# Attention and MLP block: lone score batches laid out one slot to a bank, the last v tile's products moved past the other projections, and the orders around them rewritten

## Chip, core and metric

The kernel runs on one core of one Trainium2 chip. The metric is the device time of one execution in microseconds (us). Three runs of the kernel before are given. The profile is of one further execution.

## What is computed

A block over S = 2048 tokens of width D = 640, all in float32, with adaptive LayerNorm (six vectors from `silu(c) @ w_mod`), sliding-window attention (32 heads of 20, window 256) and an MLP of width 1536. Cut to what matters:

```python
sa, ca, ga, sb, cb, gb = split(silu(c) @ w_mod)          # six vectors of 640
h = layernorm(x) * (1 + ca) + sa
q, k, v = heads(h @ wqkv)                                 # 32 heads of 20
p = softmax(where(0 <= i - j < 256, q @ k.T * 20**-0.5, -1e9))
x = x + ga * ((p @ v) @ wo)
h = layernorm(x) * (1 + cb) + sb
x = x + gb * (gelu(layernorm(h) @ w1 + b1) @ w2 + b2)
```

## The kernel before

**Numbers.** Each large product runs as three passes, high part times high part, low times high and high times low, so a float32 operand stands as two tiles, such as `hhi` and `hlo`. Making such a pair takes a copy on ScalarE (ACT) and a subtraction on GpSimd (POOL) or VectorE (DVE).

**Head.** The first two 512-token chunks are normalised, turned on TensorE (PE, tiles `psx`), scaled by `sa` and `ca1`, and the first q and k tiles are made from them (`pp`). `modulate(j)` makes `sa` and `ca1` for one fifth of the features. The string `ORDER` is the order, written out by hand, in which the head's pieces are issued: T turn, L the low part, P products, M `modulate`, S and N statistics and normalising. `run(RUN0)` is a row of dummy products (`warm`).

**The loop.** Its step t issues for one group of four heads (a quad) and one 128-query block the scores with the keys along the free axis (`s`, whose maximum gives the softmax's shift, `nm`). `LAG` = 11 steps behind it come the scores again with the queries along the free axis (`e`), a mask on DVE, the exponential on ACT (`pt`), and two zeroing selects on POOL. Two steps later follows `pt` times v (`o`, copied to `oT`). So steps 0 to 10 have an `s` batch alone, steps 11 to 127 have both, and steps 128 to 138 have an `e` batch alone. A batch is four heads of 384 columns. Two heads work on rows 0 to 63 of the PE array and two on rows 64 to 127. `score_banks` gives a batch 4 x 384 columns in three 512-column PSUM banks. So `cuts` splits the two middle heads at a bank's edge, and `score_batch` lets the second half of the array wait (a no-op with a dependence) before it writes a bank that the other half has written. Eight banks are there: three for `s`, three for `e`, one for `o`, one for `p`. Small results go "aside" into one of them.

**What fills the steps.** Between the batches stand the products of the remaining q, k and v tiles for the four chunks, 15 of 512 columns to a unit. `UNITS` is their sequence. `lay_units` spreads them so that they end by step `LAST` = 112, with a number per step that `EXTRA` shifts. Other tables place the weights' splits (`EARLY`), the asides (`AFTER`), the order of the `oT` copy against the exponential (`SUMS_LAST`) and the engine of a subtraction (`LOV`, `MV`). At step `TOMID` = 113 the projections' memory is given to the next part (`open_mid`). The output projection (`wo`) of the first four 128-row blocks stands in steps 116 to 138, placed by `TAIL_AT`. `MODS` places the sums that make the vectors ga, cb, sb and gb, on DVE, in the loop.

**Rows.** q and k go to DRAM and come back as rows of `qbuf` and `kbuf`, of which there are `NSLOT` = 4. The first rows of a quad that is due at step d are issued at step d - 7 (q) and d - 6 (k), or once they are written and their slot is free.

**MLP.** Four chunks, each 12 tiles of 128, every tile with 15 products `h`, a gelu on ACT, and 15 products `out`. The remaining 12 blocks of the output projection are placed between them.

**Issue.** All engines run their instructions in the order of the program. SyncE (SP) issues nearly all DMAs, also in program order.

## Time and profile before

| | |
|---|---|
| runs | 1003.28, 1004.44, 1005.43 us, median 1004.44 |
| the profiled execution | 1003.39 us, its span 1001.7 us |
| mean granted TensorE clock | 0.985 |
| PE busy | 952.5 us (95%) |
| DVE, POOL, ACT busy | 585.6, 495.4, 445.5 us |
| moved by DMA | 152.89 MB, mean 153 GB/s |

A row of the timeline gives start, duration, engine, operation, tiles, shape and count. In brackets is the idle time of that engine just before, and what ended it. A PE row with several instructions runs from the first start to the last end. Ends of products are modelled and overlap the next start, so what an instruction takes of PE's time is the distance from start to start. Float32 products that are not split count as two instructions. "PEclk" or "clock" is the granted share of the TensorE clock.

### The profile page before, as it was taken

Reading aid. Unit: us, or ns where it says so; the run is one execution under the profiler, and the core shown is the slowest. Engines: PE = TensorE matmul, PEld = TensorE weight load, DVE = VectorE, ACT = ScalarE, POOL = GpSimd, SP = SyncE. Lnnn points to the kernel's source line nnn. Section 1 sums busy time; section 2 is a strip of 40 time slices with the busy share of each in tenths; the row PEclk is TensorE's granted clock in tenths of the full one; section 3 lists DMA queues with packets and bytes.
Section 4 is the critical chain, followed back from the end, with each engine's and each line's share of the span. In section 5 each row is a group of like instructions: output and inputs, shape, how many; then the busy total and the mean of one; then the engine's idle time right before and its main releaser. Section 6 shows DMA issues by size and latency. Waiting matters only on the chain.

```text
span 1001.7 us, 19961 instructions
## 1 busy us (share of the span) xinstructions
PE 952.5 (95%) x7712; PEld 754.9 (75%) x7712; DVE 585.6 (58%) x929; ACT 445.5 (44%) x784; POOL 495.4 (49%) x695
## 2 busy tenths in 40 slices
PE   7899999999999999999988879999999999999997
PEld 7677677776777777777666658888888888888886
DVE  6753867768766788777778654655434343433112
ACT  3733545565654445554545554343433343333122
POOL 4323656577764355544536744454554546442221
PEclk8999999999999999999979999999999999999999
DMA  8375777655687477844582133544422334124113
GB/s 301 106 238 142 250 217 259 193 151 189 200 252 221 128 247 234 253 127 166 144 224 69 50 90 114 149 142 133 133 86 84 97 121 133 40 63 148 53 45 114
DMA packets 99429, 152.89 MB, mean 153 GB/s; under 512 B 8904, under 2 KB 42312, under 8 KB 99336
## 3 DMA queue, kind: packets, MB, share of 16 engines
q1 hardware_dynamic: 90120, 143.24, 47.0%
q10 hardware_dynamic: 9216, 8.39, 2.6%
q8 instruction: 61, 1.00, 0.4%
q14 instruction: 32, 0.26, 0.1%
HBM read 99.17 MB, written 51.58 MB: 150 GB/s over the span
## 4 chain that ended last, share of the span: by engine, by line
PE 80%; DVE 9%; ACT 5%; issue 2%; DMA 2%; POOL 1%; SPq 0%; ACTq 0%; DVEq 0%; POOLq 0%
PE h L119 16%; PE out L119 16%; PE pp L119 16%; PE o L119 7%; PE e L119 7%; PE wo L119 7%; PE s L119 6%; DVE e L119 4%; ACT pt L119 3%; DVE nm L119 2%; PE ppo L119 1%; DVE s L119 1%; PE yt L119 1%; PE xt L119 1%; DMA wc<-in_wcol 1%
## 5 line engine op out<-in xcount | busy, mean ns | idle before, releaser
L119 POOL TENSOR_SCALAR_AFFINE_SELECT pt<-pt 128x512 f32<-128x512 f32 x192 | 130.2, 678 | 148.2 <-ACT pt L119 141.6
L119 ACT ACTIVATE pt<-e 128x1024 f32<-128x1024 f32 (+1 forms) x120 | 133.8, 1115 | 54.0 <-DVE e L119 47.7
L119 DVE TENSOR_REDUCE nm<-s 128x4 f32<-128x1024 f32 (+1 forms) x128 | 152.6, 1192 | 4.4
L119 POOL TENSOR_TENSOR w2lo<-w2r,w2hi 128x640 fp32r<-128x640 f32 x48 | 75.8, 1578 | 158.2 <-ACT w2hi L119 158.0
L119 PEld LDWEIGHTS e<-qbuf,kbuf 62*128 62x128 f32 x792 | 84.9, 189 | 61.3 <-ACT pt L119 33.9
L119 PE MATMUL e<-qbuf,kbuf 62*128 62x128 f32 (+2 forms) x792 | 110.9, 319 | 19.9 <-ACT pt L119 17.2
L119 PE MATMUL pp<-hhi,whi 128*128 128x512 f32 x275 | 120.6, 439 | 2.3 <-ACT hhi L119 1.5
L119 PE MATMUL s<-kbuf,qbuf 60*128 60x256 f32 (+2 forms) x744 | 111.0, 311 | 7.5 <-DVE nm L119 5.8
L119 DVE CAST ghi<-g 128x512 fp32r<-128x512 f32 x48 | 25.8, 538 | 156.3 <-ACT g L119 156.2
L119 PE MATMUL pp<-hlo,whi 128*128 128x512 f32 x275 | 113.6, 413 | 2.4 <-POOL hlo L119 2.4
L119 DVE COPY_PREDICATED e<-mask_t,e 128x512 f32<-128x512 uint32 x96 | 66.6, 693 | 77.9 <-PE e L119 69.3
L119 PE MATMUL pp<-hhi,wlo 128*128 128x512 f32 x275 | 111.8, 407 | 0.0
L119 PE MATMUL o<-pt,vbuf 128*32 128x128 f32 x2688 | 101.7, 281 | 1.6 <-ACT xT L119 0.8
L119 POOL TENSOR_TENSOR wlo<-wraw,whi 128x128 fp32r<-128x128 f32 x185 | 81.6, 472 | 43.2 <-ACT whi L119 43.2
L119 PEld LDWEIGHTS s<-kbuf,qbuf 60*128 60x128 f32 x744 | 85.4, 188 | 19.8 <-PE pp L119 4.5
L119 ACT COPY oT<-o 128x128 f32<-128x128 f32 x128 | 33.9, 265 | 145.4 <-PE o L119 142.4
L119 PE MATMUL out<-ghi,w2hi 128*128 128x512 f32 x240 | 96.1, 400 | 0.0
L119 PE MATMUL h<-yhi,w1hi 128*128 128x512 f32 x240 | 95.6, 399 | 0.0
L119 PE MATMUL out<-ghi,w2lo 128*128 128x512 f32 x240 | 93.9, 391 | 0.0
L119 PE MATMUL out<-glo,w2hi 128*128 128x512 f32 x240 | 93.9, 391 | 0.0
L119 PE MATMUL h<-ylo,w1hi 128*128 128x512 f32 x240 | 93.8, 391 | 0.0
L119 PE MATMUL h<-yhi,w1lo 128*128 128x512 f32 x240 | 93.8, 391 | 0.0
(158 smaller groups left out, 1818.0 us busy)
## 6 DMA issues: line engine op xcount, KB each, us to landing
w2r<-in_w SPq DMA_DIRECT2D x48, 320.0 KB
qbuf<-q_scr SPq DMA_DIRECT2D x60, 240.0 KB
wraw<-in_wqkv SPq DMA_DIRECT2D x38, 320.0 KB
kbuf<-k_scr SPq DMA_DIRECT2D x44, 240.0 KB
q_scr<-stage SPq DMA_DIRECT2D x20, 512.0 KB
k_scr<-stage SPq DMA_DIRECT2D x20, 512.0 KB
o_scr<-oT ACTq DMA_DIRECT2D x64, 128.0 KB
wm<-in_wmod SPq DMA_DIRECT2D x20, 320.0 KB
```

The costliest lines, as they stand in the source:

```text
L119: return self.tc.keep_in_program_order(op(*args, **kw))
```

## The change

- **Lone batches.** Before step 11 the `s` tile, and from step 128 on the `e` tile, has four whole banks, one for each head, and no head is cut. The pools are closed and opened anew at steps 11 and 128 (`turn_scores`). Steps 11 to 127 keep three banks each.
- **The last v tile.** Its two units (30 products) leave the sequence. They run in steps 111 to 116 from the next part's memory (`late_units`). `LAST` goes from 112 to 108, `TOMID` from 113 to 110.
- **Gate.** The sums for gb leave the loop (steps 76 to 88). They stand in the first MLP chunk, with their five loads at the MLP's start (`gate`).
- **Memory.** `NSLOT` goes from 4 to 3, so the first rows of a quad are issued at step d - 5 (q) and d - 4 (k). The weights of the output projection get a pool of their own, and `yT` takes the place of `hT`.
- **Head.** `ORDER` is rewritten with further dummy products (R) in it, and `warm` goes from 31 to 61 in all, two of them in step 130 (`WARM`).
- **Tables.** `EXTRA`, `EARLY`, `AFTER`, `SUMS_LAST`, `LOV`, `HIA`, `MV`, `TAIL_AT` and others have other numbers. Four subtractions of the projections and four pairs of the modulation after the output projection go from POOL to DVE.

```diff
-NSLOT = 4
+NSLOT = 3
-RUN0 = 31
+RUN0 = 33
-    "T00 M1 S0 L00 S1 P00 S2 T01 S3 N L01 M2 T02 M3 P01 T10 T03 T11 L10 L02 M4 P02 C T04 L03 L11 P10 L04 T12 P03 T13 P11 "
+ORDER = ('T00 M1 L00 S0 S1 R12 S2 R3 S3 T01 M2 L01 P00 N T02 P01 M3 R3 T03 T10 L03 L02 M4 R1 T11 R1 R6 L10 C P02 T04 P10 ...
-LAST = 112
+LAST = 108
-EXTRA = {10: -2, 11: 2, 12: -1, 13: 1, 14: 1, 16: -3, ...
+EXTRA = {9: -2, 10: -2, 11: 6, 12: 1, 13: -1, 14: -2, ...
-MODS = [[9.25, 16.5], [18.0, 26.25], [68.5, 79.5], [76.75, 87.75]]
+MODS = [[9.5, 17.0], [16.75, 27.5], [70.5, 79.0]]
-TOMID = 113
+TOMID = 110
+WARM = {(130, 1): 2}
+LATE_AT = [110.25, 110.5, 110.5, 111.5, 113.25, 114.25, 116.5]
...
+    def turn_scores(t, n):
+        if t in (LAG, n):
+            sco_ctx.close()
+            for name in ("e", "s") if t == LAG else ("e",):
+                open_banks(name, sco_ctx)
...
-        t = pools[kind].tile([P, 4 * 384], F32, tag=kind, name=name)
-        return t, t.rearrange("p (h n) -> p h n", n=384)
+        n = width()
+        t = pools[kind].tile([P, 4 * n], F32, tag=kind, name=name)
+        return t, t.rearrange("p (h n) -> p h n", n=n)[:, :, 0:384]
+    def width():
+        return 384 if LAG <= now[0] < 2 * NQB * QUADS else 512
...
+    def late_units(key):
+        units = [unit(*key, c2, gp, acc, True) for c2 in range(2)]
+        def load():
+            w.append(box2["mid"].tile([P, KT, P], F32, tag="raw1", bufs=2, name="wraw_late"))
+            nc.sync.dma_start(w[0].rearrange("p k m -> p (k m)"), wqkv[key[1] * KT + key[2]])
+        def high():
+            nc.scalar.copy(w[1], w[0])
+        def low():
+            gp.tensor_tensor(w[2], w[0], f32(w[1]), ALU.subtract)
...
+    wm5 = [mp.tile([P, D], F32, name=f"wm5_{kt}") for kt in range(KT)]
+    for kt in range(KT):
+        nc.sync.dma_start(wm5[kt], wmod[5, kt])
+    def gate(i):
+        if i < KT:
+            mod_sum(wm5[0], wm5[i], i)
...
+            if ch == 0 and f > 1:
+                gate(f - 2)
```

Three places show what the new order does. First PE at step 2, where the `s` batch of the third query block (`s0_0_2`) stands alone between two projection units (`ppo1`, `pp0_1_1`). Before:

```order
L119 MATMUL ppo1_579<-hhi1_344,wlo001_519 128x512
L119 MATMUL s0_0_2_613<-kbuf0_97,qbuf0_93 128x256
L119 MATMUL s0_0_2_613<-kbuf0_97,qbuf0_93 128x384
L119 MATMUL s0_0_2_613<-kbuf0_97,qbuf0_93 128x128 x2
L119 MATMUL s0_0_2_613<-kbuf0_97,qbuf0_93 128x384
L119 MATMUL s0_0_2_613<-kbuf0_97,qbuf0_93 128x256
L119 MATMUL pp0_1_1_625<-hhi0_245,whi011_602 128x512
```

Now, at the same place:

```order
L119 MATMUL ppo1_602<-hhi1_371,wlo001_546 128x512
L119 MATMUL s0_0_2_636<-kbuf0_99,qbuf0_96 128x384 x4
L119 MATMUL pp0_1_1_645<-hhi0_246,whi011_625 128x512
L119 MATMUL pp0_1_1_645<-hlo0_247,whi011_625 128x512
L119 MATMUL pp0_1_1_645<-hhi0_246,wlo011_626 128x512
```

Six products became four, and the one wait inside the batch is gone. The lone `e` batches of steps 128 to 138 change in the same way. Second, PE in step 112, between the `o` products and the next `e` batch (`e1_4_6`). Before, only the turned maxima (`pm`) stand there:

```order
L119 MATMUL o1_4_2_6518<-pt1_4_1_6312,vbuf2_103 32x128 x4
L119 MATMUL o1_4_2_6518<-pt1_4_2_6362,vbuf2_103 32x128 x4
L119 MATMUL o1_4_2_6518<-pt1_4_3_6408,vbuf2_103 32x128 x4
L119 MATMUL pm1_5_6540<-idn_61,nm1_5_6054 32x128
L119 MATMUL e1_4_6_6550<-qbuf0_93,kbuf0_97 128x256
```

Now eight products of the last v tile (`pp_late`) do:

```order
L119 MATMUL o1_4_2_6467<-pt1_4_3_6358,vbuf2_104 32x128 x4
L119 MATMUL pp_late_6440<-hhi2_2369,wlo_late_6387 128x512
L119 MATMUL pp_late_6440<-hhi2_2369,whi_late_6386 128x512
L119 MATMUL pm1_5_6490<-idn_61,nm1_5_6034 32x128
L119 MATMUL pp_late_6440<-hlo2_2370,whi_late_6386 128x512
L119 MATMUL pp_late_6440<-hhi2_2369,wlo_late_6387 128x512
L119 MATMUL pp_late_6440<-hhi2_2369,whi_late_6386 128x512
L119 MATMUL pp_late_6440<-hlo2_2370,whi_late_6386 128x512
L119 MATMUL pp_late_6440<-hhi2_2369,wlo_late_6387 128x512
L119 MATMUL pp_late_6440<-hhi2_2369,whi_late_6386 128x512
L119 MATMUL e1_4_6_6506<-qbuf0_96,kbuf0_99 128x256
```

Counted over the steps in this order, the projections' products per step were 10, 5, 5, 10, 0, 0, 0, 0, 0 in steps 108 to 116. Now they are 0, 0, 0, 5, 8, 2, 5, 7, 3. Steps 11 to 107 hold 655 of them before and after. Third, SP's queue at the MLP's start, where `w1r2` and `w1r3` are raw tiles of the MLP's first weight and `w2r1` one of its second. Before:

```order
L119 DMA xb4_7757<-in_x 128x640
L119 DMA w1r2_7977<-in_w1 128x640
L119 DMA x1_scr<-xT3_7828 128x5x128
L119 DMA w1r3_7981<-in_w1 128x640
L119 DMA w2r1_7985<-in_w2 128x640
```

Now the gate's five loads, into memory that the attention's v tiles held, stand ahead of them:

```order
L119 DMA x1_scr<-xT3_7778 128x5x128
L119 DMA wm5_0_7932<-in_wmod 128x640
L119 DMA wm5_1_7933<-in_wmod 128x640
L119 DMA wm5_2_7934<-in_wmod 128x640
L119 DMA wm5_3_7935<-in_wmod 128x640
L119 DMA wm5_4_7936<-in_wmod 128x640
L119 DMA w1r2_7942<-in_w1 128x640
L119 DMA w1r3_7946<-in_w1 128x640
L119 DMA w2r1_7950<-in_w2 128x640
```

`w1r2` moved behind five loads and behind the store of `xT3`.

## The prediction

> **What bounds the kernel now.** I read the page first, for the span and TensorE's share.

> ```profile
> span 1001.7 us, 19961 instructions
> PE 952.5 (95%) x7712; PEld 754.9 (75%) x7712; DVE 585.6 (58%) x929; ACT 445.5 (44%) x784; POOL 495.4 (49%) x695
> ```

> PE is busy for 95% of the span, so time can go where PE's work shrinks, or where PE idles or runs at a lower clock. To see where that is, I read the busy time by stage. The cuts are the head in pieces, steps 0 to 10, 11 to 107, 108 to 117, 118 to 127, 128 to the loop's end, and the MLP.

> ```profile
> 12.00:24.00 12.00, 8.86 (x50) 7.47 (x50) 10.82 (x37) 4.53 (x7) 6.81 (x12) 0.72 0.97 360
> 24.00:36.00 12.00, 9.22 (x46) 6.86 (x46) 10.37 (x45) 8.85 (x13) 4.94 (x4) 0.86 0.30 69
> 47.83:98.87 51.04, 49.87 (x240) 37.03 (x241) 26.50 (x36) 17.91 (x41) 14.01 (x30) 1.00 0.60 183
> 98.87:478.71 379.84, 366.32 (x3999) 272.24 (x3998) 287.80 (x367) 202.89 (x381) 221.74 (x357) 1.00 0.68 206
> 478.71:520.07 41.36, 35.47 (x420) 27.11 (x421) 29.69 (x36) 20.59 (x39) 19.35 (x23) 0.88 0.62 174
> 520.07:559.10 39.03, 33.96 (x452) 27.66 (x452) 34.04 (x54) 19.75 (x34) 25.99 (x38) 1.00 0.34 92
> 559.10:600.96 41.86, 32.41 (x474) 24.14 (x474) 21.86 (x45) 23.57 (x42) 24.81 (x41) 0.96 0.24 71
> 600.96:1001.70 400.74, 395.51 (x1922) 334.07 (x1921) 154.51 (x288) 134.85 (x213) 169.80 (x177) 1.00 0.34 103
> ```

> Columns: length, then busy time of PE, weight loads, DVE, ACT, POOL, then the clock. Steps 0 to 10 and the MLP are PE's alone. Steps 11 to 107 leave 13.5 us of 379.84 idle. The weak places are steps 108 to 117 (5.9 us idle, clock 0.88) and everything from 559 us on to the MLP (9.5 us idle). In the head DVE is busy 21.2 of 24 us while PE's clock is low, so the low clock there is not what it waits for. The waits say who keeps PE in the loop.

> ```profile
> PE e L119 <- ACT pt L119: 17.2, 27, 2.3
> PE s L119 <- DVE nm L119: 5.8, 14, 1.3
> ```

> It is the chain e, mask, exponential, next e, since one `e` tile exists.

> **Part 1: lone batches.** A cut batch and the one lone batch that was never cut (one 128-column block per head, step 8), each with the instruction behind it, and a stretch of PE's chain for the price of a 512-column product:

> ```profile
> 57.92 0.88 PE L119 MATMUL s<-kbuf,qbuf 60*128 60x256 f32 x6
> 58.73 0.50 PE L119 MATMUL pp<-hhi,whi 128*128 128x512 f32 x1
> 87.61 0.44 PE L119 MATMUL s<-kbuf,qbuf 60*128 60x128 f32 x4
> 87.98 0.50 PE L119 MATMUL pp<-hhi,whi 128*128 128x512 f32 x1
> 931.87 3.40 PE h L119 x15
> ```

> The cut batch takes 0.81 us from start to next start, the uncut narrow one 0.37. A 512-column product takes 3.40 / 15 = 0.227 us, or 0.443 ns a column. An uncut full batch adds 256 columns per head to the narrow one. With two halves of the array at work, that is 2 x 256 x 0.443 = 0.23 us, so 0.37 + 0.23 = 0.60, a gain of 0.21. Bounds: 0.37 (a gain of 0.44) and 0.81 (none); a loss is excluded, as the columns are the same and a wait is gone. Nine batches of steps 0 to 10 were cut, PE has no idle time there, so 9 x 0.21 = **-1.9 us** (-4.0 to 0). [...]

> From step 128 on, the same batch stands in a chain. Two steps of PE, and between them ACT:

> ```profile
> 585.11 0.88 PE L119 MATMUL e<-qbuf,kbuf 62*128 62x256 f32 x6 [0.94 <-ACT pt L119]
> 588.10 0.88 PE L119 MATMUL e<-qbuf,kbuf 62*128 62x256 f32 x6 [1.31 <-ACT pt L119]
> ```
> ```profile
> 587.02 1.03 ACT L119 ACTIVATE pt<-e 128x1024 f32<-128x1024 f32 x1
> ```

> The exponential ends at 588.05 and the next `e` starts at 588.10. A step is 2.99 us, and what the batch loses the step loses. Eleven steps, of which I count eight (in the others ACT was held by the later LayerNorm, or the pieces stay small): 8 x 0.21 = **-1.7** (-2.3 to 0). Opening the pools anew makes the first `e` of steps 11 and 128 wait for the reduction that reads the old `s` tile:

> ```profile
> L119 DVE TENSOR_REDUCE nm<-s 128x4 f32<-128x1024 f32 (+1 forms) x128 | 152.6, 1192 | 4.4
> ```

> That is up to 1.2 us each, in part behind products and the `o` work: **+0.8** (0 to +2.4).

> **Part 2: the last v tile.** Steps 108 to 117 as they are, and two steps for what a step costs:

> ```profile
> 506.50 0.49 PE L119 MATMUL e<-qbuf,kbuf 62*128 62x256 f32 x4 [2.47 <-ACT oT L119]
> 507.77 1.51 PE L119 MATMUL o<-pt,vbuf 128*32 128x128 f32 x24
> 510.71 0.69 PE L119 MATMUL e<-qbuf,kbuf 62*128 62x256 f32 x3 [1.44 <-ACT pt L119]
> 517.76 0.86 PE L119 MATMUL o<-pt,vbuf 128*32 128x128 f32 x24
> ...
> 520.07 0.45 PE L119 MATMUL e<-qbuf,kbuf 62*128 62x256 f32 x3
> 523.42 0.44 PE L119 MATMUL e<-qbuf,kbuf 62*128 62x256 f32 x3
> 534.49 0.55 PE L119 MATMUL e<-qbuf,kbuf 62*128 62x128 f32 x5
> 539.07 0.50 PE L119 MATMUL e<-qbuf,kbuf 62*128 62x256 f32 x4
> ```

> After idle stretches of 2.47 and 1.44 us the clock is half, and 24 `o` products take 1.51 us instead of 0.86. Step 118, with some 1.3 us of output products, takes 3.35 us, and PE still meets the chain there. So up to six projection products are free in a step, and further ones cost 0.227 each. A step with a quad's last or first keys (step 122) takes 4.58. The new steps 108 to 117: five with up to five products at 3.35, step 112 with eight 3.35 + 2 x 0.227 = 3.8, steps 114 and 115 at 4.58, step 116 with three and six output products 3.6, step 117 at 3.35, together 36.7 against 41.36: a gain of 4.6. Steps 11 to 107 hold the same 655 products, so nothing is given back there. New waits: the raw tile's load, its copy on ACT behind the exponential, its 640-wide subtraction on POOL, and PE waits for it with the next batch queued behind. ACT and POOL take the output weights' splits in these same steps, now closer together. I put 1.1 on that: **-3.5** (-6 if the clock's loss goes wholly, +1 if the load comes a step late).

> **Part 3: the rest.** The gate's sums leave DVE in steps 76 to 88:

> ```profile
> L119 DVE SCALAR_TENSOR_TENSOR acc<-wm,sil,acc 128x640 f32<-128x640 f32 x16 | 16.7, 1046 | 0.1
> L119 DVE TENSOR_SCALAR acc<-wm,sil 128x640 f32<-128x640 f32 x4 | 2.2, 544 | 0.0
> ```

> 4 x 1.046 + 0.544 = 4.7 us go, but DVE was busy 288 of 380 us, and PE waited for it 5.8 us in the whole span: **-0.5** (-1.5 to 0). In the MLP DVE is busy 154.5 of 400.7 us, which hides them; without that cover they cost 4.7. What hangs on SP there: five loads wait for the attention's last reads, and `w1r2`, `w1r3` and `w2r1` queue behind them. ACT needs the second and third:

> ```profile
> 605.55 0.73 ACT L119 CAST w1hi<-w1r 128x640 fp32r<-128x640 f32 x1
> 606.91 0.73 ACT L119 CAST w2hi<-w2r 128x640 fp32r<-128x640 f32 x1 [0.63 <-DMA w2r<-in_w]
> ```

> ACT already waits 0.63 us there. It may wait some 2 us more, but PE has 15 second products (3.4 us) before it needs the gelu behind that: **+0.3** (0 to +2). Head: DVE's work is the same but for one subtraction, and the added dummies stand where PE waits; eight of them (16 instructions of 9.23 / 62 = 0.15 us) stand ahead of real products:

> ```profile
> 1.42 9.23 PE L119 MATMUL warm<-idn 128*128 128x128 f32 x62 [1.42 <-POOL idn masks.py:199]
> ```

> **0** (-1 to +2.4). Tables in steps 11 to 107: 13.5 us of idle can shrink or grow; **0** (-7 to +7).

> Sum: -1.9 - 1.7 + 0.8 - 3.5 - 0.5 + 0.3 = -6.5, so 1003.39 - 6.5 = **996.9 us** for an execution like the profiled one. That one was 1.05 us under the median of the runs, 1004.44.

> **The rivals.** *More from the tables.* They are fitted anew to steps without the gate's sums, and half of the 13.5 us idle goes: 996.9 - 6.8 = 990.1. For it: single steps idle over 1 us beside full ones. Against: the count of products per step hardly changed.

> *The clock drops.* Steps 108 to 110 now have no projection products at all, and the half clock after 506.50 came from such steps. It would cost what a half-clock stretch costs, some 3 us by the `o` row (0.65 us for each of three steps, and the batches): 999.9. Against: steps 135 and 136 idle 0.94 and 1.31 us of 2.99, and the stage's clock is 0.96. [...]

> [...]

> *Rows come late (slower).* With three slots a quad's first rows are issued two steps later.

> ```profile
> 224.37 2.19 SPq L119 DMA_DIRECT2D kbuf<-k_scr  x2
> ```
> ```profile
> 244.78 0.44 PE L119 MATMUL e<-qbuf,kbuf 62*128 62x256 f32 x3
> ```
> ```profile
> 64.81 2.54 DMA k_scr<-stage
> 226.66 5.66 DMA xt<-in_x
> ```
> ```profile
> SPq L119 <- POOL wlo L119: 48.0, 16, 9.2
> ```

> The k rows of the quad due at step 48 were issued 20.4 us ahead of it. Two steps of 3.9 us less leave 12.6, and two loads took 2.5 and 5.7 us to land. Some 7 us are left, less than SP's longest wait for POOL (9.2), which stands ahead of such loads in the queue. A late quad stalls `s`, and everything behind it on PE. With 13 quads so exposed, it decides from 6.5 / 13 = 0.5 us a quad; at 1 us each the time is 996.9 + 13 = 1010.

> **How the numbers follow.** A measurement of this kernel can tell about 0.2% from no change, 2.0 us: faster is below 1002.4, slower above 1006.5. Forecast 0.55 (own range 991 to 1001, from the bounds of parts 1 and 2), more from the tables 0.16, clock 0.05, lone batches 0.05, late rows 0.19. Of the first four's 0.81, 0.03 end within 0.2%, of the last 0.05. So faster 0.78, same 0.08, slower 0.14. The range leaves out the slower 0.14 and some 0.05 at its ends: 986 to 1004.

> **What would show it.** In the profile after: an uncut batch at 0.60 us from start to next start; steps 0 to 10 in 49 us; steps 108 to 117 in some 38 at full clock; a lone `e` step of 2.8; steps 11 to 107 near 380; the MLP near 401. The prediction is wrong if PE waits for `qbuf` or `kbuf` loads at a quad's first step, if `pp_late` waits for POOL, or if steps 11 to 107 change by over 7 us.

## The result, and the profile after

The changed kernel takes 1002.90 us against 1004.62 us (medians of 22 runs each on the same chip), a ratio of 0.9981 with a 95% interval of 0.9971 to 0.9991. So it gains 1.9 us (0.9 to 2.9). The forecast, 996.9 us, lies 7.5 us below the first median of before, 1004.44. The direction was right and the time lies in the stated range of 986 to 1004, but above 991 to 1001, where the forecast's own sum was put.

The profiled execution took 1004.25 us, 1.35 over the median of its kernel, while that of before was 1.05 under the median of its first three runs. So the stages below differ by 0.8 us in the wrong direction, and each is read for itself. The first lines of the page after, and its busy time by stage with the cuts of the prediction: the head, steps 0 to 10, 11 to 107, 108 to 117, 118 to 127, 128 to the first `h` product, the MLP.

```profile
span 1002.5 us, 19950 instructions
PE 951.8 (95%) x7737; PEld 755.3 (75%) x7737; DVE 592.8 (59%) x939; ACT 444.6 (44%) x781; POOL 481.7 (48%) x680
```
```profile
0.00:49.92 49.92, 42.88 (x266) 38.14 (x266) 29.69 (x108) 26.82 (x39) 20.90 (x33) 0.97 0.57 197
49.92:98.73 48.81, 47.20 (x225) 34.63 (x226) 25.81 (x34) 16.05 (x37) 13.68 (x29) 1.00 0.56 175
98.73:474.13 375.40, 363.81 (x3991) 271.07 (x3990) 283.33 (x361) 202.38 (x379) 213.06 (x350) 1.00 0.67 204
474.13:519.00 44.87, 35.00 (x419) 25.93 (x418) 30.67 (x37) 19.93 (x35) 20.01 (x22) 0.92 0.75 210
519.00:558.35 39.35, 34.61 (x456) 27.94 (x456) 33.47 (x53) 20.74 (x37) 25.46 (x38) 1.00 0.21 59
558.35:598.48 40.13, 31.25 (x460) 22.35 (x459) 22.24 (x47) 23.86 (x42) 25.26 (x42) 0.91 0.26 74
598.48:1002.50 404.02, 397.06 (x1932) 335.25 (x1931) 167.63 (x303) 134.81 (x213) 163.28 (x169) 1.00 0.34 107
```

| stage | before | after | difference | forecast |
|---|---|---|---|---|
| head | 47.83 | 49.92 | +2.1 | 0 |
| steps 0 to 10 | 51.04 | 48.81 | -2.2 | -1.9 |
| steps 11 to 107 | 379.84 | 375.40 | -4.4 | -0.5, and part of the +0.8 |
| steps 108 to 117 | 41.36 | 44.87 | +3.5 | -3.5 |
| steps 118 to 127 | 39.03 | 39.35 | +0.3 | 0 |
| 128 to first `h` | 41.86 | 40.13 | -1.7 | -1.7, and the rest of the +0.8 |
| MLP | 400.74 | 404.02 | +3.3 | +0.3 |

The two stages with lone batches fell about as forecast. The largest miss is the last v tile. SP's queue, ACT and PE where its products should start:

```profile
478.67 0.34 SPq L119 DMA_DIRECT2D cb_b<-row_scr  x1
479.06 0.57 SPq L119 DMA_DIRECT2D sb_b<-row_scr  x1
479.68 0.64 SPq L119 DMA_DIRECT2D wraw_late<-in_wqkv  x1
```
```profile
488.84 0.72 ACT L119 CAST whi_late<-wraw_late 128x640 fp32r<-128x640 f32 x1 [3.77 <-issue]
489.47 0.72 ACT L119 CAST wo_hhi<-wor 128x640 fp32r<-128x640 f32 x1
490.10 1.01 ACT L119 ACTIVATE pt<-e 128x1024 f32<-128x1024 f32 x1
```
```profile
489.62 0.50 PE L119 MATMUL pp_late<-hhi,whi_late 128*128 128x512 f32 x1 [2.73 <-ACT whi_late L119]
491.24 0.80 PE L119 MATMUL pp_late<-hhi,wlo_late 128*128 128x512 f32 x1 [0.89 <-POOL wlo_late L119]
...
494.61 1.51 PE L119 MATMUL o<-pt,vbuf 128*32 128x128 f32 x24
```

The raw tile is issued at 479.68, behind the two vectors, and ACT's copy starts 9.2 us later, after 3.77 us in which ACT stood still. The row names no releaser for this (`issue`), but in the trace ACT's queue waits from 483.48 us on for the semaphore of this load, whose last of 16 updates comes at 488.77. The other 15 have come by 487.50. The exponential is queued behind it, PE waits 2.73 us, and then the clock halves (0.50 from 490.77 to 497.59 us; the `o` row takes 1.51 us, where one at full clock, at 558.90, takes 0.86). Step 111 takes 8.5 us and step 112 6.1.

### The profile page after: what moved, and what is told of

Read it like the earlier page. It is cut to its first block, busy times and chain, and to the rows that moved or that the text cites. A ratio compares the mean times of both kernels' runs of the same rounds, so it can differ in the third digit from the quotient of the medians.

```text
span 1002.5 us, 19950 instructions
## 1 busy us (share of the span) xinstructions
PE 951.8 (95%) x7737; PEld 755.3 (75%) x7737; DVE 592.8 (59%) x939; ACT 444.6 (44%) x781; POOL 481.7 (48%) x680
## 4 chain that ended last, share of the span: by engine, by line
PE 80%; DVE 9%; ACT 4%; issue 2%; DMA 2%; POOL 1%; SPq 0%; DVEq 0%; ACTq 0%; POOLq 0%
PE pp L119 16%; PE out L119 16%; PE h L119 16%; PE o L119 7%; PE e L119 7%; PE wo L119 6%; PE s L119 6%; DVE e L119 3%; ACT pt L119 3%; DVE nm L119 2%; PE ppo L119 2%; DVE s L119 1%; PE yt L119 1%; PE pv L119 1%; PE xt L119 1%
## 5 line engine op out<-in xcount | busy, mean ns | idle before, releaser
L119 POOL TENSOR_SCALAR_AFFINE_SELECT pt<-pt 128x512 f32<-128x512 f32 x192 | 129.2, 673 | 149.3 <-ACT pt L119 142.6
L119 ACT ACTIVATE pt<-e 128x1024 f32<-128x1024 f32 (+1 forms) x120 | 133.6, 1114 | 66.6 <-DVE e L119 63.3
L119 POOL TENSOR_TENSOR w2lo<-w2r,w2hi 128x640 fp32r<-128x640 f32 x48 | 75.8, 1580 | 166.9 <-ACT w2hi L119 166.7
L119 DVE TENSOR_REDUCE nm<-s 128x4 f32<-128x1024 f32 (+1 forms) x128 | 152.7, 1193 | 4.4
L119 PEld LDWEIGHTS e<-qbuf,kbuf 62*128 62x128 f32 x773 | 81.5, 188 | 57.5 <-ACT pt L119 33.1
L119 PE MATMUL e<-qbuf,kbuf 62*128 62x128 f32 (+2 forms) x773 | 108.0, 320 | 17.3 <-ACT pt L119 17.0
L119 PE MATMUL s<-kbuf,qbuf 60*128 60x128 f32 (+2 forms) x728 | 108.3, 312 | 10.3 <-DVE nm L119 7.4
L119 PE MATMUL pp<-hhi,whi 128*128 128x512 f32 x265 | 114.0, 430 | 0.9 <-ACT whi L119 0.7
L119 DVE COPY_PREDICATED e<-mask_t,e 128x512 f32<-128x512 uint32 x96 | 66.6, 694 | 77.5 <-PE e L119 66.8
L119 DVE CAST ghi<-g 128x512 fp32r<-128x512 f32 x48 | 27.1, 565 | 143.9 <-ACT g L119 143.8
L119 PE MATMUL pp<-hlo,whi 128*128 128x512 f32 x265 | 107.6, 406 | 3.1 <-POOL hlo L119 3.1
L119 PE MATMUL pp<-hhi,wlo 128*128 128x512 f32 x265 | 108.2, 408 | 0.0
L119 PE MATMUL o<-pt,vbuf 128*32 128x128 f32 x2688 | 102.1, 282 | 0.5 <-ACT oT L119 0.4
L119 PEld LDWEIGHTS s<-kbuf,qbuf 60*128 60x128 f32 x728 | 82.9, 187 | 21.7 <-DVE nm L119 5.4
L119 POOL TENSOR_TENSOR wlo<-wraw,whi 128x128 fp32r<-128x128 f32 x180 | 77.9, 463 | 39.9 <-ACT whi L119 32.0
L119 PE MATMUL out<-ghi,w2hi 128*128 128x512 f32 x240 | 96.2, 401 | 0.0
L119 PE MATMUL h<-yhi,w1hi 128*128 128x512 f32 x240 | 95.8, 399 | 0.0
L119 PE MATMUL out<-ghi,w2lo 128*128 128x512 f32 x240 | 94.1, 392 | 0.0
L119 PE MATMUL out<-glo,w2hi 128*128 128x512 f32 x240 | 94.0, 392 | 0.0
L119 PE MATMUL h<-ylo,w1hi 128*128 128x512 f32 x240 | 93.9, 391 | 0.0
L119 PE MATMUL h<-yhi,w1lo 128*128 128x512 f32 x240 | 93.9, 391 | 0.0
L119 ACT COPY oT<-o 128x128 f32<-128x128 f32 x128 | 33.8, 264 | 128.2 <-PE o L119 121.8
```

Of the source, the lines that this page charges most:

```text
L119: return self.tc.keep_in_program_order(op(*args, **kw))
```

## The experiments

Each kernel is compared with the kernel before on the same chip; e1 to e4, e5 to e8 and e9 to e12 ran on three different ones. Within one program the stages repeat to some 0.2 us where the clock is the same (steps 108 to 117 of e2 and e9, the same program there: 42.16 and 42.18 us, both at 0.80), so a stage shows more than a total.

### The changed kernel again (e1)

> The changed kernel once more, unaltered, as the control of this group and for a second profile. Theory A (the late tile's load lands after the exponentials need ACT, so ACT's copy holds the exponential and PE stalls in step 111): the stall of about 4 us in step 111 is there again, steps 108 to 117 take 44 to 46 us, about 1003 us in all. Theory B (the stall belongs to that one execution, whose time was 1.35 us over the median of its runs): the stall is under 2 us, steps 108 to 117 take under 42.5.

1003.22 us, ratio 0.9987 (0.9977 to 0.9997). The stall in step 111 is there again (4.1 us), and steps 108 to 117 take 44.8 us. So theory A holds: the stall does not belong to that one execution.

### The last v tile back among the projections (e2)

```diff
-    *seq, _, (last, _) = [k for nm in UNITS for k in pairs(*nm)]
+    seq = [k for nm in UNITS for k in pairs(*nm)]
-TOMID = 110
+TOMID = 113
```

The times of the splits of the output weights behind step 109 and of the MLP's first weights are those of before again, and the asides from step 104 on follow no table.

> The last v tile goes back into the projections' sequence (8, 7, 7, 8 products in steps 108 to 111), the projections' memory is given away at step 113 again; steps 11 to 107 hold the same products as in the changed kernel. Theory A: steps 108 to 117 fall from 44.9 to about 41 us, so 3.5 to 4 us less in all, 999 us. Theory B: 1002 to 1004 us, as the changed kernel. Theory C (steps 108 to 117 are held by the chain of e, mask, exponential whatever PE has to do there): steps 108 to 117 stay at 44 to 45 us, the idle time only moves to steps 112 to 115.

999.57 us, ratio 0.9955 (0.9941 to 0.9969). The stage:

```profile
473.84:516.00 42.16, 37.16 (x421) 28.48 (x420) 30.07 (x37) 20.21 (x37) 18.11 (x21) 0.80 0.70 193
```

2.7 us less than in the changed kernel, and the median is 3.7 us below that of e1 on the same chip. Theory A holds, with less gain in the stage than expected, as 17 us of it run at half clock (by the mean of 0.80 over 42.16 us). The stage is no shorter than before (42.16 against 41.36).

### The late tile's load ahead of the two vectors (e3)

```diff
-        nc.sync.dma_start(box2["cb"], row_scr[1])
-        nc.sync.dma_start(box2["sb"], row_scr[2])
+    def vectors():
+        nc.sync.dma_start(box2["cb"], row_scr[1])
+        nc.sync.dma_start(box2["sb"], row_scr[2])
+    spread(plan, [step(1, vectors)], 112.5, 112.75)
```

> The load of the late raw tile goes ahead of the two broadcast vectors cb and sb (320 KB each), which are loaded at step 112.5 instead; nothing else moves. Theory A: the load lands about 2 us earlier (two of some six tiles ahead of it are gone), the stall in step 111 falls from 4.0 to about 2 us, the total by 2 to 3 us. Theory C: no change of the stages beyond 1 us.

999.74 us, ratio 0.9957 (0.9944 to 0.9971). The stage, the load and the copy on ACT:

```profile
473.85:515.56 41.71, 34.73 (x418) 25.58 (x417) 31.11 (x37) 19.82 (x35) 20.15 (x22) 0.92 0.78 213
```
```profile
478.07 0.39 SPq L119 DMA_DIRECT2D wraw_late<-in_wqkv  x1
```
```profile
485.18 0.73 ACT L119 CAST whi_late<-wraw_late 128x640 fp32r<-128x640 f32 x1 [0.38 <-issue]
```

The copy starts 3.7 us earlier, ACT's wait falls from 3.77 to 0.38 us, and PE's idle time in step 111 from 4.0 to 1.1. The order of three loads was worth 3.2 us in this stage, so theory A holds, with more gain than it put. Even so the late tile is no gain over before (41.71 against 41.36).

### The late tile's copy and products a step later (e4)

```diff
-LATE_AT = [110.25, 110.5, 110.5, 111.5, 113.25, 114.25, 116.5]
+LATE_AT = [110.25, 112.0, 112.0, 112.75, 114.0, 114.75, 116.75]
```

> The load stays where it is, but the late tile's copy on ACT moves from step 110.5 to 112.0 and its products from steps 111.5 to 116.5 to steps 112.75 to 116.75. Theory A: ACT no longer waits for the load ahead of an exponential, the stall goes wholly, steps 108 to 117 take 39 to 41 us, 4 to 6 us less in all. Theory C: steps 108 to 117 stay at 43 to 45 us, as steps 108 to 112 then have no products at all and each costs the chain's 3.5 us, and the products are paid in full behind them.

1010.99 us, ratio 1.0078 (1.0060 to 1.0095), and steps 108 to 117 take 50.4 us. Neither theory gave that. PE's waits:

```profile
493.06 0.50 PE L119 MATMUL pp_late<-hhi,whi_late 128*128 128x512 f32 x1 [1.84 <-ACT whi_late L119]
495.58 0.80 PE L119 MATMUL pp_late<-hhi,wlo_late 128*128 128x512 f32 x1 [1.79 <-POOL wlo_late L119]
507.82 0.67 PE L119 MATMUL pp_late<-hhi,whi_late 128*128 128x512 f32 x1 [2.63 <-ACT vT L119]
```
```profile
491.37 1.02 ACT L119 ACTIVATE pt<-e 128x1024 f32<-128x1024 f32 x1 [0.48 <-DVE e L119]
492.29 0.72 ACT L119 CAST whi_late<-wraw_late 128x640 fp32r<-128x640 f32 x1
```

ACT no longer waits for the load. But the products follow the copy too closely: PE waits for ACT behind the exponential, for POOL behind two selects, and the second unit waits for ACT to empty the one bank that both use. So the load was one wait of a chain, and a later place in itself brings nothing.

### The uncut lone batches alone (e5)

The kernel before with `score_banks`, `width`, `cuts`, `turn_scores` and `aside` of the changed kernel.

> The kernel before with the uncut lone batches alone (four whole banks before step 11 and from step 128 on). Theory A (each term of the lone batches as predicted): steps 0 to 10 fall from 51.0 to about 49 us, step 128 to the first h product from 41.9 to about 40, opening the pools anew costs under 1 us, 1001 us in all. Rival: the gains seen in the changed kernel's steps 0 to 10 come from its other tables; then these stages change by under 0.7 us and the time stays at 1004.

999.95 us, ratio 0.9950 (0.9935 to 0.9964): more than the whole change. Steps 0 to 10 and 128 to the first `h`, and the batch of step 2 of the changed kernel with the instruction behind it:

```profile
50.52:99.22 48.70, 47.22 (x224) 34.59 (x225) 25.82 (x34) 17.23 (x39) 14.39 (x31) 1.00 0.63 193
...
556.08:595.64 39.56, 29.75 (x455) 21.07 (x455) 21.47 (x45) 23.75 (x42) 24.73 (x41) 0.96 0.26 75
```
```profile
58.96 0.62 PE L119 MATMUL s<-kbuf,qbuf 60*128 60x384 f32 x4
59.51 0.50 PE L119 MATMUL pp<-hhi,whi 128*128 128x512 f32 x1
```

Both stages fell by 2.3 us, as in theory A. A batch takes 0.55 us. The head is 2.7 us longer in this execution, 1.2 of it in PE's longer wait for the `wc` load (2.8 us against 1.6). Another 1.2 is new: the first `s` batch waits 1.41 us for a DVE copy. The same wait in the changed kernel:

```profile
49.92 0.44 PE L119 MATMUL s<-kbuf,qbuf 60*128 60x128 f32 x4 [1.45 <-DVE stage L119]
```

### The head in its old order (e6)

```diff
-ORDER = ('T00 M1 L00 S0 S1 R12 ...
+ORDER = ( "T00 M1 S0 L00 S1 P00 ...
-RUN0 = 33
+RUN0 = 31
```

> The changed kernel with the head's old order (ORDER, RUN0, LOWP of the kernel before, 62 dummy instructions instead of 114 in the head). Theory A (the new order of the head costs 2.1 us of itself): the head falls from 49.9 to 47.8 us, the total by about 2 us. Rival (the other changes make the head longer, as the memory handed out anew, or the new order is made up for in steps 0 to 10): the head stays at 49.9, or steps 0 to 10 get longer by as much, and the time stays at 1003.

1003.56 us, ratio 0.9990 (0.9978 to 1.0002). `LOWP` goes back too. Theory A falls: the median does not drop by 2 us, and the head takes 51.5 us, not 47.8.

```profile
0.00:51.53 51.53, 43.39 (x211) 37.49 (x211) 28.29 (x109) 27.03 (x39) 19.47 (x32) 0.80 0.56 191
```

The clock is 0.80 in it, with the new order 0.97. This execution, 1006.76 us, was the slowest of its twelve, so its head alone says little. But over the traces the nine heads in the new order take 49.3 to 50.4 us, and the three in the old order with uncut lone batches (e5, e6, e12) 50.5 to 51.5. So the new order costs nothing and rather helps, by about 1 us, which the totals cannot tell from nothing.

### Before without the gate (e7)

```diff
-            mod_col(ps, box["acc"])
-            nc.vector.tensor_copy(gb, ps)
+            nc.vector.tensor_copy(gb, b2_sb)
```

> The kernel before without the gate's sums: the five loads, the five sums on DVE and the ten products pmc for the vector gb are left out, so gb has other values; its place in the order is else the same. Theory A (the 4.4 us that steps 11 to 107 gained are the tables'): steps 11 to 107 fall by the 1.2 us of the products and at most 0.5, to about 378.2 us. Rival (DVE's 4.7 us of sums held the chain): they fall by 3.5 to 4.5, to about 375.8 us.

1002.68 us, ratio 0.9981 (0.9971 to 0.9990). Steps 11 to 107 take 379.88 us, as before, but with two stretches of half clock in them instead of one (the second, from 238.38 us on, at 0.50). So neither number came. Step by step against before, steps 45 to 47, with the second stretch, are 0.65 us longer, and steps 87 and 88 are 0.8 us shorter. In step 87 stood the ten products `pmc`. Steps 77 to 86, over which DVE's sums were spread, changed by less than 0.05 us each, so the rival, that these sums held the chain, falls.

### The gate's loads behind the MLP's first tiles (e8)

```diff
-    for kt in range(KT):
-        nc.sync.dma_start(wm5[kt], wmod[5, kt])
+            if ch == 0 and f == 1:
+                for kt in range(KT):
+                    nc.sync.dma_start(wm5[kt], wmod[5, kt])
```

> The changed kernel with the gate's five loads issued behind the raw tiles w1r3 and w2r2, in the second of the MLP's twelve tiles, the sums where they were. Theory A (the loads hold the MLP's first raw tiles back on SP, so ACT's copies, the gelu and DVE's sums come late and PE waits 1.2 us): the MLP falls from 404.1 to about 402.5 us; the 1.7 us of the ten products and their wait stay. Rival (the gate's sums on DVE hold PE): the MLP stays at 404 us.

1002.52 us, ratio 0.9975 (0.9962 to 0.9987), and the MLP takes 402.3 us, as theory A has it. ACT's second copy and the gelu behind it in the changed kernel, then PE's wait, then the copy in this one:

```profile
607.92 0.73 ACT L119 CAST w2hi<-w2r 128x640 fp32r<-128x640 f32 x1 [2.79 <-DMA w2r<-in_w]
608.56 0.68 ACT L119 ACTIVATE g<-h,b_sb 128x512 f32<-128x512 f32 x1
```
```profile
611.77 0.41 PE L119 MATMUL wo<-wo_hhi,ot 128*128 128x320 f32 x1 [1.23 <-DVE xb L119]
```
```profile
601.69 0.73 ACT L119 CAST w2hi<-w2r 128x640 fp32r<-128x640 f32 x1 [0.69 <-DMA w2r<-in_w]
```

PE's wait of 1.23 us is gone, and the MLP is 1.7 us shorter. The total shows it less clearly: its interval overlaps that of the changed kernel (0.9971 to 0.9991). The wait also differs between executions: in e3, with the loads in their old place and the loop's end 0.8 us longer, PE does not meet it, and the MLP takes 402.6 us. What `xb` waited for in the changed kernel is DVE's row ahead of it:

```profile
609.27 1.31 DVE L119 CAST ghi<-g 128x512 fp32r<-128x512 f32 x1 [3.27 <-ACT g L119]
610.62 0.69 DVE L119 TENSOR_TENSOR glo<-g,ghi 128x512 fp32r<-128x512 f32 x1
611.23 0.48 DVE L119 TENSOR_TENSOR xb<-wo,xb 128x320 f32<-128x320 f32 x1
```

The 1.6 us that are left over before are the ten products that turn the sum into a column, and their wait:

```profile
670.28 1.28 PE L119 MATMUL pmc<-ones,wm 128*128 128x1 f32 x10 [0.35 <-ACT xT L119]
```

Steps 108 to 117, whose program is that of the changed kernel, took another course in this execution:

```profile
474.74:516.29 41.55, 37.47 (x417) 28.09 (x416) 30.69 (x37) 20.02 (x35) 19.95 (x22) 0.84 0.82 228
```

The clock was half from 478.8 us on, PE came to the late products later and met no stall there (0.15 us idle in step 111). So the same program takes 41.6 to 44.9 us in this stage. That this is part of why the changed kernel's median is better than its profile is likely, but not shown. Among its 22 runs the three with a mean clock of 0.985 took 1000.6 to 1001.1 us and the four with 0.990 took 1003.5 to 1004.9, which fits. The twelve runs of e1 show no such order. The five runs of e3 lie between 999.05 and 1000.59.

### Both repairs, then dummies, then other banks (e9, e10, e11)

e9 joins the edits of e2 and e8. e10 adds dummies to it, and e11 opens the pool for small results ahead of the scores' pool:

```diff
-WARM = {(130, 1): 2}
+WARM = {(111, 3): 2, (112, 3): 4, (113, 3): 3, (114, 3): 5, (115, 3): 4, (130, 1): 2, (135, 3): 4, (136, 3): 4, (137, 3): 6}
```
```diff
-("o", att_ctx, "right"), ("s", sco_ctx, "right"), ("a", sco_ctx, "right")
+("o", att_ctx, "right"), ("a", sco_ctx, "right"), ("s", sco_ctx, "right")
```

> The changed kernel with both repairs: the last v tile back among the projections, the gate's loads behind the MLP's first raw tiles. Theory (the misses are independent and add up): steps 108 to 117 take 41 to 42.5 us, the MLP 402.3, the rest as in the changed kernel; 3.7 + 1.5 us less, about 998 us, ratio to the kernel before near 0.993. Rival (one repair gives back what the other brought): 1000 us or more.

> As the last one, with dummy products of 128 columns at the ends of steps 111 to 115 (2, 4, 3, 5, 4) and 135 to 137 (4, 4, 6), where PE waits for the exponential. Theory D (the clock is decided on a grid of 3.41 us, and falls to half behind a window in which PE was busy for less than some 0.6): no half-clock stretch between 480 and 580 us, steps 108 to 117 take 39 to 40 us, step 128 to the first h product 38 to 39, 3 to 5 us less than without the dummies. Rival (the chain sets these steps at either clock, and dummies only take PE's time): these stages stay within 1 us or grow.

> As e9, with the pool for small results opened ahead of the four-bank pool of the scores, so that the first score batch gets other banks. Theory E (the first lone batch waits 1.4 us at the head's end, since its fourth bank is one that DVE's copy to the stage tile still reads): the wait of the first s batch for DVE's stage goes, the head is 1 to 1.4 us shorter. Rival (all the banks that are left are read as late as that one): the wait stays at 1.4 us.

e9: 1000.03 us, 0.9957 (0.9942 to 0.9971). The MLP takes 402.5 us, but the total is that of e2: the 1.3 us are below what the runs can tell, so 1000.03 meets the rival's 1000 or more only by number. It is also no better than e5, the lone batches alone (0.9950). So with both misses repaired, the rest of the change (head, tables, memory) brings nothing that the totals can tell. e10: 998.38 us, 0.9937 (0.9923 to 0.9951). e11: 997.99 us, 0.9949 (0.9933 to 0.9965). Its ten runs form two groups, six from 996.87 to 998.09 and four from 1001.43 to 1002.91, so the ratio of the medians, 0.9931, flatters it. The wait of 1.4 us at the head's end stays, so theory E falls as put. e10 and e11 beat both kernels, e9 just, but none the others by more than the intervals. Steps 108 to 117 of e9, e10 and e11:

```profile
473.91:516.09 42.18, 37.20 (x422) 28.59 (x422) 30.10 (x37) 20.20 (x37) 18.10 (x21) 0.80 0.70 194
```
```profile
474.75:514.75 40.00, 36.23 (x458) 28.58 (x458) 30.19 (x37) 19.97 (x37) 18.10 (x21) 1.00 0.70 196
```
```profile
473.65:513.70 40.05, 33.70 (x421) 25.81 (x420) 30.09 (x37) 20.21 (x37) 18.11 (x21) 0.91 0.71 202
```

With the dummies the clock stayed at 1.00 in this stage, which is 2.2 us shorter than in e9. But e11 has the same program here as e9 and takes as little as e10, at a clock of 0.91, so the gain in time is not shown to be the dummies'. In the lone `e` steps they did not help (40.8 us against 40.5), and the total fell by 1.7 us, not by 3 to 5. So theory D holds for the clock of the first stage alone. Over the runs the mean clock is 0.993 to 0.996 in all six of e10, 0.979 to 0.988 in the six of e9, and 0.980 to 0.983 in the four long runs of e11 against 0.993 in its six others.

### The lone batches without the gate (e12)

e5 and e7 in one kernel.

> The kernel before with the uncut lone batches and without the gate's loads, sums and products (gb has other values, as in e7). With no half-clock stretch in steps 11 to 107, these took 377.7 us in e5 and 375.4 in the changed kernel. Theory F (the gate's part of the loop makes all of this difference, the renewed tables none): 375.2 to 376.0 us. Rival (the tables bring 1 us or more of it): 376.4 to 377.2 us. A half-clock stretch of 3.4 us would add some 2 us and has to be read off the clock first.

```profile
99.45:477.07 377.62, 365.01 (x3988) 270.99 (x3988) 283.53 (x361) 202.49 (x381) 219.32 (x356) 1.00 0.66 202
```

Step by step against e5, two places differ. Steps 45 to 47 are 0.8 us longer, with a half-clock stretch at 237.4 us that e5 has not. Steps 87 and 88 are 0.8 us shorter, without the products `pmc`. So without the stretch it would be 376.9 us, an estimate from this one execution, in the rival's range, and theory F falls by this reading. It rests on the 0.8 us read from the steps: with the 2 us put on a stretch beforehand, it would be 375.6, in theory F's range. e7 against before gives nearly the same pair, 0.65 longer and 0.8 shorter.

## Why the prediction was wrong, step by step

**The last v tile (-3.5 forecast, +3.5 measured) is the step that failed.** It counted steps by the products in them. The terms for steps 108 to 110 and 113 to 117 were right to within 0.3 us but one (step 116, 4.8 instead of 3.6), but step 111 was put at 3.35 and took 8.47, and step 112 at 3.8 and took 6.09: together 7.4 us, more than the whole miss. The part named the right queue (load, ACT's copy, POOL's subtraction, PE behind them) and put 1.1 us on it. One of its signs of being wrong came: `pp_late` waited 0.89 us for POOL, though 2.73 us for ACT's copy ahead of that. Its bound of +1 for a late load was too narrow, as the two vectors ahead of the load, 640 KB, were not counted, and neither was the half clock behind the stall (6.83 us). Moving these two behind the load took 3.2 us off the stage (e3).

**Lone batches (-1.9 and -1.7).** Right in mechanism and nearly in size: 0.55 us a batch against 0.60, stages 2.2 and 1.7 us shorter, and 2.3 each in e5. Part of a batch's time does not go with its columns: the narrow batch of step 8 still takes 0.37 us, and its columns alone, 2 x 128 at 0.443 ns, come to 0.11 by estimate. What that part is, no run here shows. That the stage comes out so near is in part luck. Nine batches of steps 0 to 10 lost 0.24 to 0.33 us each, some 2.4 together. Step 0 also lost a wait of 0.7 us for `whi`. Against that, the faster steps meet a wait of 0.9 us for DVE's write of `kbuf` at the end of step 3, and in step 10 one of 0.7 for `whi`. The wait put on reopening the pools (+0.8) did not come in the changed kernel: no `e` batch of steps 11 and 128 waits for `nm`. The first batch waits instead, for DVE's copy to `stage`. Why it does is open, since other banks did not change it.

**Gate.** In the loop -0.8 us (e12, e7), inside the forecast's -1.5 to 0, but by luck: it was put on DVE's sums, and it came from the products `pmc`. In the MLP +3.3 where +0.3 was put: 1.7 from the loads on SP (e8), within its range of 0 to 2. The cover named, PE's 15 second products, did hold, but DVE's late `ghi` delayed `xb`, for which PE's `wo` products wait. Another 1.6 are the `pmc` products and the wait ahead of them, which the sum never moved from the loop to the MLP.

**Tables (0).** Steps 11 to 107 are 4.4 us shorter. By differences between single executions, 1.25 are the half-clock stretch at step 34, which e5 has not either, and some 0.9 more came with the lone batches (2.2 in e5 in all). 0.8 are the gate's. That leaves 1.5 for the tables and the rest of the change, inside their bounds; which of them brought it, no run shows.

**Head (0).** +2.1 between the two executions. The first batch's wait is 1.3 of it, against which step 0 loses a wait of 0.7 us. The new order of itself costs nothing, as far as these heads show (e6). In the old order the head takes 47.8 and 48.3 us without uncut lone batches (before, e7) and 50.5 to 51.5 with them. What makes this difference beyond the 1.3 us stays open.

**The rivals.** Late q and k rows: refuted. These are PE's two longest waits in steps 11 to 107 of the changed kernel (us, times, longest); none is for a `qbuf` or `kbuf` load.

```profile
PE s L119 <- DVE nm L119: 6.2, 11, 1.3
PE e L119 <- ACT pt L119: 4.3, 8, 0.8
```

The clock: steps 108 to 110 passed in the changed kernel's two profiles (in the first, three windows of 3.41 us from 477.11 us on with PE busy 63% of the time, all at 1.00), but in e8, with the same three steps, the clock was half from 478.8 us on. Lone batches that gain nothing (put at 0.05): refuted, as both their stages fell by 2.3 us in e5. More from the tables: some 1.5 us by the differences above, not 6.8.

## What to carry to other kernels

A step priced by its products is priced only if their operands are there. Follow a moved piece of work back to its load and count the bytes queued ahead of it: one reordering of three loads (3.2 us in its stage) was worth more than the whole change (1.9). Where parts of a change can be run alone, do so, since here the simplest part brought more than all of them together.

## What the runs showed of the hardware

In the windows of this grid between 50 and 980 us the two traces show this. PE's busy time is worked out from the products' records, whose ends are modelled. Of the windows at full clock, four have PE busy for 22 to 41% of the time, and each is followed by a half-clock window. Of ten with 58 to 65% it is one, and of 18 with 65 to 76% none. The windows ahead of the stretches named in e7 and e9, with PE busy 1.92 and 1.90 of 3.41 us (56%), are at full clock too. A window of before, the one behind it, and one of the changed kernel that passed:

```profile
186.64:190.05 3.41, 2.09 (x33) 1.29 (x31) 3.31 (x7) 2.81 (x4) 1.50 (x4) 1.00 0.49 156
190.05:193.47 3.42, 3.42 (x9) 2.31 (x11) 2.10 (x4) 0.89 (x2) 2.98 (x5) 0.50 0.59 147
```
```profile
214.29:217.70 3.41, 2.13 (x33) 1.52 (x24) 3.07 (x5) 2.44 (x4) 0.38 (x1) 1.00 0.04 10
```

PE idles 1.3 us in each of the two windows. The one, 61% busy, is followed by half clock, the other, 62% busy, is not, nor is one of the changed kernel that is 59% busy (2.01 us at 582.93). So the 0.6 of theory D parts these windows only roughly, and what decides between them is not shown. One half-clock window in the loop cost 0.65 to 1.6 us, by steps: 0.65 and 0.75 in steps 45 to 47 (e7, e12), 1.2 in step 34 (e10, before) and 1.6 in step 42 (e6). So the same stall costs this much more in some executions and not in others, which is likely part of why runs of one kernel differ, those of before by 5 us (1001.92 to 1007.13).
